# Gate normalisation in PSUM, factor sums on GpSimd, and stored outputs gated one behind each addition

## The chip, the cores and the metric

One NeuronCore of a Trainium2 chip runs the whole program in one launch. The metric is the device time in microseconds; three runs of the kernel before took 2028.3, 2031.29 and 2031.46 us, so the median is 2031.29 us. Each engine works through its own queue in order: TensorE (PE: matmuls, and PEld: loads of its weights), VectorE (DVE), ScalarE (ACT), GpSimd (POOL) and SyncE (SP, which issues all DMAs here). Results of matmuls land in PSUM, which GpSimd cannot be given as an operand here; everything else is in SBUF.

## The reference

Attention in which every query keeps its 32 largest scores, and on its output a mixture of 8 experts. The weights of the experts for each token come from a matrix that is normalised over rows and columns in turn, 8 times (Sinkhorn), so every token uses every expert, and no expert's share is known before the last token's attention is done.

```python
scores = scale * q @ k.T                      # 4 batches, 8 heads, 576 x 576, head size 64
kth = np.partition(scores, -32)[..., -32]     # keep the 32 largest of a row
attn = softmax(where(scores >= kth, scores, -1e9))
x = (attn @ v) as 2304 x 512
P = np.exp(x @ w_gate - max)                  # 2304 x 8
for _ in range(8):
    P /= P.sum(1, keepdims=True) + 1e-09
    P /= P.sum(0, keepdims=True) + 1e-09
    P *= N / E
for e in range(8):
    out += P[:, e:e + 1] * (np.maximum(x @ w1[e], 0.0) @ w2[e])   # w1: 512 x 1024, w2: 1024 x 512
```

## The kernel before

The tokens form 18 tiles of 128 rows. Tiles 0 to 9 (five blocks, `BOARD`) go through the experts while attention for later tokens still runs; since the gate is not known yet, their 80 outputs (10 tiles, 8 experts) are copied to DRAM by `output` without their gate factor. Tiles 10 to 17 (`LAST`) go through the experts after attention. All matmuls of the experts work on values split in two: a high half rounded to the matmul's format (`hi_act`, on ScalarE) and a low half, the difference (`lo_pool` on GpSimd or `lo_dve` on VectorE), in three products: high by high, high by low, low by high. Every weight tile, 128 x 1024, is loaded by SP (`wr`), its high half `wh` made by ScalarE and its low half `wl` by GpSimd.

When the last attention stage is done, `gate_logits` has left all logits in `lg`, and `sinkhorn` makes `P` of them, 128 partitions x 18 tiles x 8 experts: the row sums and both divisions are VectorE's, the sum over the 128 partitions is a matmul with a matrix of ones into PSUM (line 381). Then the PSUM and SBUF pools of attention are closed, and those of the last phase (`psx`, `x2`, `h2`, `cp_`) take their place, so the first matmuls into `pb` and `pc` come after the last round.

`right_factors` prepares the last 8 tiles for a product of 2 x 2 blocks with seven products instead of eight (Strassen's scheme in Winograd's form): B11, B21, B22 are blocks of x, T1 to T4 are differences of blocks, 512 columns x 2 each, and each of the seven is split into halves. `left_factors` does the same to each w1 tile: four sums S1 to S4 on GpSimd (line 593), and the split of the tile and of the sums.

The last phase is 16 half visits, two for each expert. A half visit is two `hidden_pair` (seven products of 6 matmuls, line 607, then ReLU and the split of h into `h2h` and `h2l`) and `last_outputs`: for each of the 8 tiles, 12 matmuls (line 666) into a `p2` bank, of which there are two, and an addition on VectorE, `acc = p2 * P + acc` (line 515, the first time line 513). After each of the half visits 2 to 11, `finish` takes one of tiles 0 to 9: eight times it loads a stored output into a `y` slot (there are four, `YB`) and adds it to an `acc` in the same way, then it stores the `acc`.

The order on each engine is made by a scheduler ahead of the run: it takes the program as traced, the priorities (`tc.high_priority`) and its own model of durations, and lists each engine's instructions; on the chip each queue runs in that order and waits at semaphores. So `finish` can be moved up by it, ahead of what was traced before, as soon as its operands exist.

Of the kernel before, what the change touches and what calls it, by code (L numbers as in the profile page):

```python
# [7 lines left out]
F32 = mybir.dt.float32  # L8
F32R = mybir.dt.float32r
AF = mybir.ActivationFunctionType  # L10
OP = mybir.AluOpType
# [3 lines left out]
DM, E, F = 512, 8, 1024  # L15
N = NB * S
NT = N // 128
# [10 lines left out]
BLOCKS = [[("t", b, 2 * p), ("t", b, 2 * p + 1)] for b in range(NB) for p in range(2)]  # L28
# [3 lines left out]
BOARD = [0, 4, 8, 12, 16]  # L32
# [7 lines left out]
WR, WB, XR, NS, RAW, YB = 3, 6, 3, 3, 3, 4  # L40
# [3 lines left out]
def kernel(  # L44
# [11 lines left out]
    nc = tc.nc  # L56
# [3 lines left out]
    const = ctx.enter_context(tc.tile_pool(name="const", bufs=1))  # L60
    wp = ctx.enter_context(tc.tile_pool(name="wp", bufs=2))
    op_ = ctx.enter_context(tc.tile_pool(name="op", bufs=2))
# [6 lines left out]
    pss = actx.enter_context(tc.tile_pool(name="pss", bufs=1, space=PSUM))  # L69
    pst = actx.enter_context(tc.tile_pool(name="pst", bufs=2, space=PSUM))  # L70
# [3 lines left out]
    def hi_act(dst, src):  # L74
        nc.scalar.activation(dst, src, AF.Copy)  # L75
# [4 lines left out]
    def lo_pool(dst, src, hi):  # L80
        nc.gpsimd.tensor_tensor(dst, src, hi.bitcast(F32), op=OP.subtract)  # L81

    def lo_dve(dst, src, hi):
        nc.vector.tensor_tensor(dst, src, hi.bitcast(F32), op=OP.subtract)  # L84
# [8 lines left out]
    P = const.tile([128, NT, E], F32, name="P")  # L93

    tile_id = {p: i for i, p in enumerate(p for blk in BLOCKS for p in blk)}

    def store_rows(eng, src, piece):
        kind, a, b = piece
        if kind == "t":
            r = a * S + b * 128  # L100
            eng.dma_start(out[r:r + 128, :], src)
        else:
            for i, bb in enumerate((a, b)):
                r = bb * S + 512
                eng.dma_start(out[r:r + 64, :], src[i * 64:(i + 1) * 64])

    spill = {}
# [251 lines left out]
    ones = const.tile([128, 128], F32, name="ones")  # L359
    nc.vector.memset(ones, 1.0)  # L360

    def sinkhorn():
        lgf = lg.rearrange("p t e -> p (t e)")
        mx = const.tile([128, 1], F32, name="mx")
        nc.vector.reduce_max(mx, lgf, axis=mybir.AxisListType.X)
        tp = pst.tile([128, 512], F32, name="pt")
        nc.tensor.transpose(tp[:, 0:128], mx.to_broadcast([128, 128]), idt)
        nmx = const.tile([128, 1], F32, name="nmx")
        nc.vector.reduce_max(nmx, tp[:, 0:128], axis=mybir.AxisListType.X)
        nc.vector.tensor_scalar(nmx, nmx, -1.0, None, op0=OP.mult)  # L370
        nc.scalar.activation(P.rearrange("p t e -> p (t e)"), lgf, AF.Exp, bias=nmx)
        rs = const.tile([128, NT], F32, name="rs")
        cs = const.tile([128, E], F32, name="cs")
        for _ in range(8):
            nc.vector.reduce_sum(rs, P, axis=mybir.AxisListType.X)
            nc.vector.tensor_scalar(rs, rs, 1e-9, None, op0=OP.add)
            nc.vector.reciprocal(rs, rs)
            nc.vector.tensor_tensor(P, P, rs[:, :, None].to_broadcast([128, NT, E]), op=OP.mult)
            nc.vector.reduce_sum(cs, P.rearrange("p t e -> p e t"), axis=mybir.AxisListType.X)
            cp = pst.tile([128, 512], F32, name="pt")  # L380
            nc.tensor.matmul(cp[:, 0:E], ones, cs, start=True, stop=True)
            cr = const.tile([128, E], F32, name="cr")
            nc.vector.tensor_scalar(cr, cp[:, 0:E], 1e-9, None, op0=OP.add)
            nc.vector.reciprocal(cr, cr)
            nc.vector.tensor_scalar(cr, cr, float(N // E), None, op0=OP.mult)
            nc.vector.tensor_tensor(P, P, cr[:, None, :].to_broadcast([128, NT, E]), op=OP.mult)

    ACC = {}

# [119 lines left out]
    def add_output(t, y, e):  # L509
        g = P[:, t, e:e + 1]  # L510
        if t not in ACC:
            ACC[t] = cp_.tile([128, 512], F32, name="acc", bufs=10)
            nc.vector.tensor_scalar(ACC[t], y, g, None, op0=OP.mult)
        else:
            nc.vector.scalar_tensor_tensor(ACC[t], y, g, ACC[t], op0=OP.mult, op1=OP.add)  # L515

    def finish(pieces):
        for piece in pieces:
            t = tile_id[piece]
            for e in range(E):  # L520
                y = op_.tile([128, 512], F32, name="y", bufs=YB)
                nc.sync.dma_start(y, spill[t, e])
                add_output(t, y, e)
            store_rows(nc.sync, ACC[t], piece)

    def right_factors(tm):
        def rows(kh):

            for c, (a, b) in enumerate(((5, 7), (6, 8))):
                cs = slice(c * 256, c * 256 + 256)
                x1 = block_rows(a)[:, 2 * kh:2 * kh + 2, :]
                if BLOCKS[b][0][0] == "t":
                    yield cs, x1, block_rows(b)[:, 2 * kh:2 * kh + 2, :]
                else:
                    for i, piece in enumerate(BLOCKS[b]):
                        ms = slice(c * 256 + i * 128, c * 256 + i * 128 + 128)
                        yield ms, x1[:, :, i * 128:i * 128 + 128], X[piece][:, 2 * kh:2 * kh + 2, :]

        def block_rows(blk):
            x = X[BLOCKS[blk][0]]
            return bass.AP(tensor=x.tensor, offset=x.offset, ap=[list(p) for p in x.ap[:-1]] + [[1, 256]])

        def factor(name):
            return [x2.tile([128, 2, 512], F32R, name=f"{name}{p}", bufs=1) for p in "hl"]

        def split(name, parts):
            h, l = factor(name)
            for cs, src in parts:  # L550
                hi_act(h[:, :, cs], src)
                lo_dve(l[:, :, cs], src, h[:, :, cs])
            return h, l

        def temp():
            return tm.tile([128, 2, 512], F32, name="tf", bufs=4)

        def sub(dst, a, b):
            nc.vector.tensor_tensor(dst, a, b, op=OP.subtract)

        top, low = list(rows(0)), list(rows(1))
        f = {}
        f["B11"] = split("B11", [(cs, a) for cs, a, _ in top])
        t1, t2 = temp(), temp()
        for cs, a, b in top:
            sub(t1[:, :, cs], b, a)
        f["T1"] = split("T1", [(slice(0, 512), t1)])
        f["B21"] = split("B21", [(cs, a) for cs, a, _ in low])
        for cs, _, b in low:
            sub(t2[:, :, cs], b, t1[:, :, cs])  # L570
        f["T2"] = split("T2", [(slice(0, 512), t2)])
        t3 = temp()
        for (cs, _, b1), (_, _, b2) in zip(top, low):
            sub(t3[:, :, cs], b2, b1)
        f["T3"] = split("T3", [(slice(0, 512), t3)])
        f["B22"] = split("B22", [(cs, b) for cs, _, b in low])
        t4 = temp()
        for cs, a, _ in low:
            sub(t4[:, :, cs], a, t2[:, :, cs])
        f["T4"] = split("T4", [(slice(0, 512), t4)])  # L580
        return f
# [72 lines left out]
        put(1, 0, u)  # L654
        return hh, hl

    def last_outputs(e, s0, hs):
        ws = [convert(w2[e, s0 + i], [128, 2, 512]) for i in range(2)]
        for ti, piece in enumerate(p for blk in LAST for p in BLOCKS[blk]):
            ts = slice(ti * 128, ti * 128 + 128)  # L660
            ps = ps2.tile([128, 512], F32, name="p2")
            i = 0
            for (hh, hl), (wh, wl) in zip(hs, ws):
                for ft in range(2):
                    for a, m in ((hh, wh), (hh, wl), (hl, wh)):
                        nc.tensor.matmul(ps, a[:, ft, ts], m[:, ft, :], start=(i == 0), stop=(i == 11))  # L666
                        i += 1
            add_output(tile_id[piece], ps, e)
            if e == E - 1 and s0 == 2:
                store_rows(nc.sync, ACC[tile_id[piece]], piece)  # L670

# [2 lines left out]
    factors = {}  # L674
# [23 lines left out]
    first.close()  # L698
    h2 = ctx.enter_context(tc.tile_pool(name="h2", bufs=3))
    cp_ = ctx.enter_context(tc.tile_pool(name="cp", bufs=2))  # L700
    spilled = [p for blk in range(len(BOARD)) for p in BLOCKS[blk]]
    for e in range(E):
        for s0 in (0, 2):
            last_outputs(e, s0, [hidden_pair(e, s0 + i, factors) for i in range(2)])
            if 2 * e + s0 // 2 >= 2:
                finish(spilled[:1])
                del spilled[:1]


# [55 lines left out]
```

## Time and profile before

| | us |
|---|---|
| median of three runs | 2031.29 |
| lowest, highest | 2028.3, 2031.46 |
| the profiled execution | 2030.8 |
| its span, first to last instruction | 2029.0 |
| TensorE busy | 1901.4 |
| VectorE busy | 1534.8 |
| GpSimd busy | 1079.9 |
| ScalarE busy | 1045.0 |

The profile is one execution. Its rows call the engines PE, PEld, DVE, ACT, POOL and SP; `L515` is line 515 of the kernel; `acc<-y,P,acc` names output and inputs of an instruction; `x70` is a count. `<-` in a list of waits reads "waited for". PEclk is the clock that TensorE was granted as a share of full speed, 2.4 GHz.

### The profile page before, as it was taken

Reading aid. Unit: us, or ns where it says so; the run is one execution under the profiler, and the core shown is the slowest. Engines: PE = TensorE matmul, PEld = TensorE weight load, DVE = VectorE, ACT = ScalarE, POOL = GpSimd, SP = SyncE. Lnnn points to the kernel's source line nnn. Section 1 sums busy time; section 2 is a strip of 40 time slices with the busy share of each in tenths; the row PEclk is TensorE's granted clock in tenths of the full one; section 3 lists DMA queues with packets and bytes.
Section 4 is the critical chain, followed back from the end, with each engine's and each line's share of the span. In section 5 each row is a group of like instructions: output and inputs, shape, how many; then the busy total and the mean of one; then the engine's idle time right before and its main releaser. Section 6 shows DMA issues by size and latency. Waiting matters only on the chain.

```text
span 2029.0 us, 27288 instructions
## 1 busy us (share of the span) xinstructions
PE 1901.4 (94%) x9571; PEld 1586.7 (78%) x9571; DVE 1534.8 (76%) x2861; ACT 1045.0 (52%) x1715; POOL 1079.9 (53%) x953
## 2 busy tenths in 40 slices
PE   4798789999999999999999999879889999999998
PEld 3676678888888887878888888667668888888887
DVE  8999999999999999946999993857893333333333
ACT  5766667657656656645656666423222333333331
POOL 4547866655545544535545556834444454355530
PEclk9899989999999999999999999989899999999999
DMA  3476545443333333324333335414661111111111
GB/s 112 143 246 222 186 165 165 150 155 115 107 124 120 115 114 107 120 102 156 113 106 119 118 115 167 135 52 150 215 205 42 46 59 63 42 42 52 63 42 42
DMA packets 95785, 238.97 MB, mean 118 GB/s; under 512 B 10784, under 2 KB 12960, under 8 KB 95648
## 3 DMA queue, kind: packets, MB, share of 16 engines
q1 hardware_dynamic: 95648, 237.23, 36.3%
q8 instruction: 75, 1.23, 0.3%
q14 instruction: 62, 0.51, 0.1%
HBM read 203.11 MB, written 34.08 MB: 117 GB/s over the span
## 4 chain that ended last, share of the span: by engine, by line
PE 52%; DVE 38%; DMA 5%; issue 3%; ACT 1%; POOL 1%; SPq 0%; DVEq 0%; ACTq 0%; POOLq 0%
PE p L666 15%; DVE m L136 11%; PE p L497 10%; DVE w L143 9%; PE p L410 9%; PE p L607 7%; DVE Et L145 5%; PE pc L607 4%; DVE hl L460 3%; DVE acc L515 3%; DVE atl L84 2%; PE pb L607 2%; DMA y<-y 2%; DMA wr<-in_w_dram 1%; PE pt L233 1%
## 5 line engine op out<-in xcount | busy, mean ns | idle before, releaser
L81 POOL TENSOR_TENSOR wl<-wr,wh 128x1024 fp32r<-128x1024 f32 x280 | 687.5, 2466 | 531.5 <-ACT wh L75 522.5
L75 ACT ACTIVATE wh<-wr 128x1024 fp32r<-128x1024 f32 x280 | 294.3, 1059 | 254.0 <-PE p L607 164.5
L136 DVE MAX8 m<-w 128x8 f32<-128x576 f32 x432 | 318.5, 750 | 1.7
L410 PE MATMUL p<-xh,wh 128*128 128x256 f32 (+1 forms) x768 | 265.6, 346 | 14.8 <-DVE hl L460 8.5
L410 PE MATMUL p<-xl,wh 128*128 128x256 f32 (+1 forms) x768 | 262.7, 342 | 0.0
L410 PE MATMUL p<-xh,wl 128*128 128x256 f32 (+1 forms) x768 | 262.3, 342 | 0.0
L497 PE MATMUL p<-wh,hl 128*128 128x512 f32 x640 | 249.0, 400 | 9.6 <-DVE hl L460 9.6
L497 PE MATMUL p<-wh,hh 128*128 128x512 f32 x640 | 253.5, 400 | 0.5 <-ACT hh L459 0.5
L497 PE MATMUL p<-wl,hh 128*128 128x512 f32 x640 | 251.9, 397 | 0.5 <-POOL wl L81 0.5
L666 PE MATMUL p<-wh,h2h 128*128 128x512 f32 x512 | 203.5, 397 | 12.1 <-DVE acc L515 11.4
L143 DVE MATCH_REPLACE8 w<-m,w 128x576 f32<-128x576 f32 x288 | 213.8, 744 | 0.2
L666 PE MATMUL p<-wh,h2l 128*128 128x512 f32 x512 | 199.3, 395 | 6.7 <-DVE h2l L631 6.7
L666 PE MATMUL p<-wl,h2h 128*128 128x512 f32 x512 | 201.9, 394 | 0.0
L515 DVE SCALAR_TENSOR_TENSOR acc<-p,P,acc 128x512 f32<-128x512 f32 x120 | 88.7, 749 | 147.6 <-PE p L666 147.6
L145 DVE SCALAR_TENSOR_TENSOR Et<-s,m,Et 128x576 f32<-128x576 f32 x144 | 164.2, 1148 | 17.0 <-ACT Et L139 16.2
L410 PEld LDWEIGHTS p<-xh,wh 128*128 128x128 f32 x768 | 147.4, 192 | 36.9 <-DVE hl L460 9.4
L410 PEld LDWEIGHTS p<-xl,wh 128*128 128x128 f32 x768 | 147.5, 192 | 14.5
L410 PEld LDWEIGHTS p<-xh,wl 128*128 128x128 f32 x768 | 147.5, 192 | 14.5 <-issue 0.4
L497 PEld LDWEIGHTS p<-wh,hl 128*128 128x128 f32 x640 | 121.0, 190 | 34.1 <-DVE hl L460 11.6
L497 PEld LDWEIGHTS p<-wl,hh 128*128 128x128 f32 x640 | 121.9, 191 | 24.1 <-POOL wl L81 0.9
L497 PEld LDWEIGHTS p<-wh,hh 128*128 128x128 f32 x640 | 121.8, 191 | 23.6 <-ACT hh L459 1.4
L152 ACT ACTIVATE Et<-Et,st 128x576 f32<-128x576 f32 x144 | 105.0, 771 | 57.4 <-DVE st L150 57.2
(179 smaller groups left out, 4105.2 us busy)
## 6 DMA issues: line engine op xcount, KB each, us to landing
wr<-in_w_dram SPq DMA_DIRECT2D x240, 512.0 KB, 3.5
y<-y SPq DMA_DIRECT2D x160, 256.0 KB, 3.1
raw<-in_k_dram SPq DMA_DIRECT2D x56, 288.0 KB, 3.1
wr<-in_w_dram SPq DMA_DIRECT2D x48, 256.0 KB, 3.5
raw<-in_q_dram SPq DMA_DIRECT2D x32, 256.0 KB, 3.0
p<-y SPq DMA_DIRECT2D x32, 256.0 KB, 3.3
y<-p SPq DMA_DIRECT2D x32, 256.0 KB, 4.1
raw<-in_v_dram SPq DMA_DIRECT2D x28, 288.0 KB, 2.9
```

Source lines behind the costliest of these rows:

```text
L75: nc.scalar.activation(dst, src, AF.Copy)
L81: nc.gpsimd.tensor_tensor(dst, src, hi.bitcast(F32), op=OP.subtract)
L136: nc.vector.max(m8[u][:, r, :], ws[u] if r else s)
L143: nc.vector.match_replace(ws[u], m8[u][:, r, :], ws[u] if r else s, LOWEST)
L145: nc.vector.scalar_tensor_tensor(Em, s, m8[u][:, 3, 7:8], Em, op0=OP.is_ge, op1=OP.mult, accum_out=rsum)
L152: nc.scalar.activation(Et[:, i, :], Et[:, i, :], AF.Copy, scale=st[:, 1, i:i + 1])
L410: nc.tensor.matmul(ps[:, fo, :], a[:, kk, fs], x[:, k0 + kk, cs], start=(i == 0), stop=(i == 3 * nk - 1))
L460: nc.vector.scalar_tensor_tensor(seat.hl[:, ft, cs], src, 0.0, seat.hh[:, ft, cs].bitcast(F32), op0=OP.max, op1=OP.subtract)
L497: nc.tensor.matmul(ps, a[:, ft, ts], m[:, ft % 2, :], start=(i == 0), stop=(i == 3 * NFT - 1))
L515: nc.vector.scalar_tensor_tensor(ACC[t], y, g, ACC[t], op0=OP.mult, op1=OP.add)
L607: nc.tensor.matmul(ps, w[:, kk, :], x[:, kk, :], start=(fresh and i == 0), stop=(i == 5), skip_group_check=True)
L666: nc.tensor.matmul(ps, a[:, ft, ts], m[:, ft, :], start=(i == 0), stop=(i == 11))
```

## The change

There are three parts. (1) `sinkhorn` keeps the gate matrix, the row sums and the scaled column sums in one PSUM tile, `bank`, the one that held attention scores; the reciprocals `rs` and `cr` and the partial sums `cs` stay in SBUF. The addition of 1e-9 and the factor N/E become one instruction, so a round has eight instructions on VectorE instead of nine. The last round writes `P` in SBUF. (2) In `right_factors` the differences and all low halves go from VectorE to GpSimd. (3) `finish` becomes a generator, `stored`, which gives one stored output at each call; `last_outputs` calls it after each of its additions, and `tc.issue_after` makes the VectorE instruction of that call come after the addition in VectorE's queue. So ten half visits, from the first, gate 8 stored outputs each.

```diff
--- before.py
+++ after.py
@@ -368,22 +368,25 @@
         nmx = const.tile([128, 1], F32, name="nmx")
         nc.vector.reduce_max(nmx, tp[:, 0:128], axis=mybir.AxisListType.X)
         nc.vector.tensor_scalar(nmx, nmx, -1.0, None, op0=OP.mult)
-        nc.scalar.activation(P.rearrange("p t e -> p (t e)"), lgf, AF.Exp, bias=nmx)
+
+        bank = pss.tile([128, 2, 512], F32, name="sp")
+        Q = bank[:, 0, 0:NT * E].rearrange("p (t e) -> p t e", t=NT)
+        rp, cp = bank[:, 0, 256:256 + NT], bank[:, 0, 320:320 + E]
+        nc.scalar.activation(bank[:, 0, 0:NT * E], lgf, AF.Exp, bias=nmx)
         rs = const.tile([128, NT], F32, name="rs")
         cs = const.tile([128, E], F32, name="cs")
-        for _ in range(8):
-            nc.vector.reduce_sum(rs, P, axis=mybir.AxisListType.X)
-            nc.vector.tensor_scalar(rs, rs, 1e-9, None, op0=OP.add)
-            nc.vector.reciprocal(rs, rs)
-            nc.vector.tensor_tensor(P, P, rs[:, :, None].to_broadcast([128, NT, E]), op=OP.mult)
-            nc.vector.reduce_sum(cs, P.rearrange("p t e -> p e t"), axis=mybir.AxisListType.X)
-            cp = pst.tile([128, 512], F32, name="pt")
-            nc.tensor.matmul(cp[:, 0:E], ones, cs, start=True, stop=True)
-            cr = const.tile([128, E], F32, name="cr")
-            nc.vector.tensor_scalar(cr, cp[:, 0:E], 1e-9, None, op0=OP.add)
-            nc.vector.reciprocal(cr, cr)
-            nc.vector.tensor_scalar(cr, cr, float(N // E), None, op0=OP.mult)
-            nc.vector.tensor_tensor(P, P, cr[:, None, :].to_broadcast([128, NT, E]), op=OP.mult)
+        cr = const.tile([128, E], F32, name="cr")
+        for i in range(8):
+            nc.vector.reduce_sum(rp, Q, axis=mybir.AxisListType.X)
+            nc.vector.tensor_scalar(rp, rp, 1e-9, None, op0=OP.add)
+            nc.vector.reciprocal(rs, rp)
+            nc.vector.tensor_tensor(Q, Q, rs[:, :, None].to_broadcast([128, NT, E]), op=OP.mult)
+            nc.vector.reduce_sum(cs, Q.rearrange("p t e -> p e t"), axis=mybir.AxisListType.X)
+            ct = pst.tile([128, 512], F32, name="pt")
+            nc.tensor.matmul(ct[:, 0:E], ones, cs, start=True, stop=True)
+            nc.vector.tensor_scalar(cp, ct[:, 0:E], 1e-9, float(E) / N, op0=OP.add, op1=OP.mult)
+            nc.vector.reciprocal(cr, cp)
+            nc.vector.tensor_tensor(P if i == 7 else Q, Q, cr[:, None, :].to_broadcast([128, NT, E]), op=OP.mult)
 
     ACC = {}
 
@@ -510,18 +513,19 @@
         g = P[:, t, e:e + 1]
         if t not in ACC:
             ACC[t] = cp_.tile([128, 512], F32, name="acc", bufs=10)
-            nc.vector.tensor_scalar(ACC[t], y, g, None, op0=OP.mult)
-        else:
-            nc.vector.scalar_tensor_tensor(ACC[t], y, g, ACC[t], op0=OP.mult, op1=OP.add)
-
-    def finish(pieces):
-        for piece in pieces:
-            t = tile_id[piece]
-            for e in range(E):
-                y = op_.tile([128, 512], F32, name="y", bufs=YB)
-                nc.sync.dma_start(y, spill[t, e])
-                add_output(t, y, e)
-            store_rows(nc.sync, ACC[t], piece)
+            return nc.vector.tensor_scalar(ACC[t], y, g, None, op0=OP.mult)
+        return nc.vector.scalar_tensor_tensor(ACC[t], y, g, ACC[t], op0=OP.mult, op1=OP.add)
+
+
+    def stored(piece):
+        t = tile_id[piece]
+        for e in range(E):
+            y = op_.tile([128, 512], F32, name="y", bufs=YB)
+            nc.sync.dma_start(y, spill[t, e])
+            add_output(t, y, e)
+            if e == E - 1:
+                store_rows(nc.sync, ACC[t], piece)
+            yield
 
 
 
@@ -549,14 +553,14 @@
             h, l = factor(name)
             for cs, src in parts:
                 hi_act(h[:, :, cs], src)
-                lo_dve(l[:, :, cs], src, h[:, :, cs])
+                lo_pool(l[:, :, cs], src, h[:, :, cs])
             return h, l
 
         def temp():
             return tm.tile([128, 2, 512], F32, name="tf", bufs=4)
 
         def sub(dst, a, b):
-            nc.vector.tensor_tensor(dst, a, b, op=OP.subtract)
+            nc.gpsimd.tensor_tensor(dst, a, b, op=OP.subtract)
 
         top, low = list(rows(0)), list(rows(1))
         f = {}
@@ -654,7 +658,7 @@
         put(1, 0, u)
         return hh, hl
 
-    def last_outputs(e, s0, hs):
+    def last_outputs(e, s0, hs, more):
         ws = [convert(w2[e, s0 + i], [128, 2, 512]) for i in range(2)]
         for ti, piece in enumerate(p for blk in LAST for p in BLOCKS[blk]):
             ts = slice(ti * 128, ti * 128 + 128)
@@ -665,7 +669,9 @@
                     for a, m in ((hh, wh), (hh, wl), (hl, wh)):
                         nc.tensor.matmul(ps, a[:, ft, ts], m[:, ft, :], start=(i == 0), stop=(i == 11))
                         i += 1
-            add_output(tile_id[piece], ps, e)
+            added = add_output(tile_id[piece], ps, e)
+            with tc.issue_after(added.ins):
+                next(more, None)
             if e == E - 1 and s0 == 2:
                 store_rows(nc.sync, ACC[tile_id[piece]], piece)
 
@@ -698,13 +704,10 @@
     first.close()
     h2 = ctx.enter_context(tc.tile_pool(name="h2", bufs=3))
     cp_ = ctx.enter_context(tc.tile_pool(name="cp", bufs=2))
-    spilled = [p for blk in range(len(BOARD)) for p in BLOCKS[blk]]
+    more = (x for blk in range(len(BOARD)) for p in BLOCKS[blk] for x in stored(p))
     for e in range(E):
         for s0 in (0, 2):
-            last_outputs(e, s0, [hidden_pair(e, s0 + i, factors) for i in range(2)])
-            if 2 * e + s0 // 2 >= 2:
-                finish(spilled[:1])
-                del spilled[:1]
+            last_outputs(e, s0, [hidden_pair(e, s0 + i, factors) for i in range(2)], more)
 
 
 # ---- launch: one core; inputs laid out for the kernel, output as the reference has it ----
```

GpSimd's queue around the new work. Before, from the last splits of weights (`wl`) for the visits to the first sums (line 593) and splits for `hidden_pair`:

```order
L81 TENSOR_TENSOR wl<-wr,wh 128x1024 x18
L593 TENSOR_TENSOR wr<-wr 128x256 x2
L81 TENSOR_TENSOR wl<-wr,wh 128x1024
L593 TENSOR_TENSOR wr<-wr 128x256 x5
L81 TENSOR_TENSOR wl<-wr,wh 128x1024 x2
```

The same place now, where `tf` are the differences and line 597 is what 593 was; ahead of these rows stand two differences and the low halves of B11, B21 and most of B22:

```order
L81 TENSOR_TENSOR T1l<-tf,T1h 128x1024
L81 TENSOR_TENSOR B22l<-xm,B22h 128x2x128
L81 TENSOR_TENSOR wl<-wr,wh 128x1024 x3
L563 TENSOR_TENSOR tf<-xt,tf 128x2x256
L81 TENSOR_TENSOR T3l<-tf,T3h 128x1024
L563 TENSOR_TENSOR tf<-xt,tf 128x2x128 x2
L81 TENSOR_TENSOR T2l<-tf,T2h 128x1024
L81 TENSOR_TENSOR wl<-wr,wh 128x1024 x3
L81 TENSOR_TENSOR T4l<-tf,T4h 128x1024
L81 TENSOR_TENSOR wl<-wr,wh 128x1024 x3
L597 TENSOR_TENSOR wr<-wr 128x256 x7
L81 TENSOR_TENSOR wl<-wr,wh 128x1024 x2
```

The last nine weight splits ahead of the sums now stand behind and between the factor work; two of the five sums that stood behind the first split for `hidden_pair` now stand ahead of the second.

VectorE's queue in the finishing stretch. Before, where additions of stored outputs (`acc<-y`) begin to stand among those of the current half visit (`acc<-p`):

```order
L515 SCALAR_TENSOR_TENSOR acc<-y,P,acc 128x512 x3
L515 SCALAR_TENSOR_TENSOR acc<-p_14332,P,acc 128x512
L515 SCALAR_TENSOR_TENSOR acc<-y,P,acc 128x512
L636 TENSOR_TENSOR pb<-p_14419,t 128x512
L513 TENSOR_SCALAR acc<-y,P 128x512
L515 SCALAR_TENSOR_TENSOR acc<-y,P,acc 128x512 x2
```

Now, in the second half visit:

```order
L517 SCALAR_TENSOR_TENSOR acc<-p_14302,P,acc 128x512
L516 TENSOR_SCALAR acc<-y,P 128x512
L517 SCALAR_TENSOR_TENSOR acc<-p_14320,P,acc 128x512
L517 SCALAR_TENSOR_TENSOR acc<-y,P,acc 128x512
L640 TENSOR_TENSOR pc<-pc,t 128x512
L640 TENSOR_TENSOR pb<-pb,t 128x512
L635 SCALAR_TENSOR_TENSOR h2l<-pc,h2h 128x512
L517 SCALAR_TENSOR_TENSOR acc<-p_14337,P,acc 128x512
L517 SCALAR_TENSOR_TENSOR acc<-y,P,acc 128x512
```

Stored and current additions alternate, one to one, in the first ten half visits.

SP's queue. Before, in the finishing stretch, loads of stored outputs (`y`) and the store of a finished tile (line 101) follow each other with few weight loads between; afterwards weight loads (`wr`) come in pairs:

```order
L522 DMA y<-y_7_13820 128x512
L392 DMA wr<-in_w_dram 128x1024
L101 DMA out_dram<-acc 128x512
L585 DMA wr<-in_w_dram 128x1024 x2
L392 DMA wr<-in_w_dram 128x1024 x2
```

Now, one of the ten half visits, where line 589 loads a w1 tile and line 395 a w2 tile:

```order
L524 DMA y<-y_4_4674 128x512
L524 DMA y<-y_5_5018 128x512
L524 DMA y<-y_6_5362 128x512
L524 DMA y<-y_7_5706 128x512
L524 DMA y<-y_0_7920 128x512
L524 DMA y<-y_1_8204 128x512
L589 DMA wr<-in_w_dram 128x1024
L524 DMA y<-y_2_8488 128x512
L101 DMA out_dram<-acc 128x512
L524 DMA y<-y_3_8772 128x512
L395 DMA wr<-in_w_dram 128x1024 x2
L589 DMA wr<-in_w_dram 128x1024
```

The weight loads of these half visits stand among loads that wait for a `y` slot, and two of them behind a store that waits for the eighth addition of a stored output.

On TensorE's queue the eight column sums move up among the last visits; the second, third and fourth of them stand in a row, behind two matmuls of a group whose third needs the low half of its weights.

## Rows read from the trace of the kernel before

**Rows 1.** The page, parts 1 and 2: busy shares; TensorE and its clock in 40 slices.

```profile
PE 1901.4 (94%) x9571; PEld 1586.7 (78%) x9571; DVE 1534.8 (76%) x2861; ACT 1045.0 (52%) x1715; POOL 1079.9 (53%) x953
...
PE   4798789999999999999999999879889999999998
...
PEclk9899989999999999999999999989899999999999
```

**Rows 2.** Busy time by stretch: stretch, its length, then each engine with its instruction count.

```profile
1262.40:1340.00 77.60, 56.27 (x291) 48.00 (x291) 64.06 (x110) 30.49 (x45) 50.54 (x27) 0.85 0.33 111
...
1390.00:1520.00 130.00, 112.52 (x439) 86.76 (x438) 117.46 (x135) 34.79 (x51) 58.04 (x36) 0.92 0.69 218
...
1600.00:2000.00 400.00, 400.00 (x1740) 326.15 (x1739) 149.73 (x214) 131.50 (x190) 185.27 (x128) 1.00 0.14 47
```

**Rows 3.** Who waited for whom, 1388 to 1530 us: total, times, longest, in us.

```profile
PE p L666 <- DVE acc L515: 10.7, 8, 2.8
PE p L666 <- DVE h2l L631: 6.7, 3, 3.4
```

**Rows 4.** Instruction groups of VectorE, 1388 to 1520 us: count, busy us, mean ns, idle before.

```profile
L515 DVE SCALAR_TENSOR_TENSOR acc<-y,P,acc 128x512 f32<-128x512 f32 x70 | 79.5, 1138 | 9.6 <-DMA y<-y 8.4 <-DVE h2l L631 0.3
L515 DVE SCALAR_TENSOR_TENSOR acc<-p,P,acc 128x512 f32<-128x512 f32 x18 | 13.2, 744 | 0.0
```

**Rows 5.** VectorE in order of time, from 1388 us: start, duration in us.

```profile
1391.04 2.31 DVE L515 SCALAR_TENSOR_TENSOR acc<-y,P,acc 128x512 f32<-128x512 f32 x1
```

**Rows 6.** Who waited for whom, 1262 to 1340 us, waits of TensorE.

```profile
PE pt L381 <- DVE cs L379: 13.2, 4, 4.0
PE p L497 <- DVE hl L460: 5.7, 1, 5.7
PE p L410 <- DVE hl L460: 2.1, 1, 2.1
```

**Rows 7.** Matmuls of line 607 alone, in three stretches.

```profile
1312.00:1320.00 8.00, 4.57 (x18) 3.18 (x18) 0.94 0.91 276
1320.00:1332.50 12.50, 0.00 (x0) 0.00 (x0) 0.50 0.18 68
1332.50:1340.00 7.50, 7.45 (x24) 5.64 (x24) 0.76 0.00 0
```

**Rows 8.** Busy time in two short stretches of the transition.

```profile
1273.30:1279.00 5.70, 0.00 (x0) 0.00 (x0) 5.70 (x4) 0.54 (x1) 5.70 (x3) 0.92 0.25 92
1279.00:1284.50 5.50, 5.47 (x13) 4.31 (x14) 5.50 (x3) 1.58 (x2) 4.12 (x2) 0.50 0.65 200
```

**Rows 9.** GpSimd in order of time, 1255 to 1335 us.

```profile
1261.80 2.41 POOL L81 TENSOR_TENSOR wl<-wr,wh 128x1024 fp32r<-128x1024 f32 x1 [1.88 <-ACT wh L75]
1267.26 15.86 POOL L81 TENSOR_TENSOR wl<-wr,wh 128x1024 fp32r<-128x1024 f32 x4 [3.06 <-ACT wh L75]
...
1322.31 2.95 POOL L593 TENSOR_TENSOR wr<-wr 128x256 f32<-128x256 f32 x4
```

**Rows 10.** VectorE in order of time, 1262 to 1334 us.

```profile
1272.72 3.18 DVE L84 TENSOR_TENSOR T1l<-tf,T1h 128x1024 fp32r<-128x1024 f32 x1
...
1284.79 1.21 DVE L84 TENSOR_TENSOR T2l<-tf,T2h 128x1024 fp32r<-128x1024 f32 x1
...
1299.74 0.17 DVE L383 TENSOR_SCALAR cr<-pt 128x8 f32<-128x8 f32 x1 [0.54 <-PE pt L381]
...
1300.18 2.23 DVE L385 TENSOR_SCALAR cr<-cr 128x8 f32<-128x8 f32 x1
...
1329.69 0.31 DVE L386 TENSOR_TENSOR P<-P,cr 128x144 f32<-128x144 f32 x1
...
1332.96 0.31 DVE L386 TENSOR_TENSOR P<-P,cr 128x144 f32<-128x144 f32 x1
```

**Rows 11.** The page, parts 5 and 6: weight halves on ScalarE; DMA issue to landing, us.

```profile
L75 ACT ACTIVATE wh<-wr 128x1024 fp32r<-128x1024 f32 x280 | 294.3, 1059 | 254.0 <-PE p L607 164.5
...
wr<-in_w_dram SPq DMA_DIRECT2D x240, 512.0 KB, 3.5
y<-y SPq DMA_DIRECT2D x160, 256.0 KB, 3.1
```

## The prediction

> **What bounds the kernel now.** I read the page's busy shares and slices first, then the stretches, then who waited for whom, then the timelines of the engines waited for. The page shows a kernel bound by TensorE: busy 94% of 2029.0 us, its clock at full speed in nearly every slice, so a gain can only come from where TensorE stands or runs slow [rows 1]. Two places near the gate are such.
>
> The first is the finishing stretch, 1390 to 1520 us, in which `finish` adds the 80 stored outputs. From 1600 to 2000 us TensorE retires 1740 matmuls in 400 us, 4.35 per us, without a gap; this is the same mixture of `hidden_pair` and `last_outputs`, without stored outputs. From 1390 to 1520 it retires 439 where that rate gives 565.5 [rows 2]. The 126.5 missing ones are 126.5 / 4.35 = 29.1 us: 17.5 us idle (130 - 112.52), the other 11.6 us at a granted clock of 0.92 on average. The waits name VectorE, 10.7 us for the additions that free the `p2` banks and 6.7 us for the low halves of h [rows 3]. VectorE is 90% busy there (117.46 of 130), because 70 of the additions take 1138 ns each, against 744 ns for those that read PSUM [rows 2, 4].
>
> The second is the transition, 1262 to 1340 us, from the last gate logits to the first full `hidden_pair`. TensorE does 56.3 us of work in 77.6 us: 21.3 us idle [rows 2]. It waits 5.7 and 2.1 us for the low half of h, which stands on VectorE behind the factor sums, and 13.2 us for the column sums of the Sinkhorn rounds [rows 6]. 18 matmuls of line 607 are done by 1320 us, none in the next 12.5 us, then 24 in 7.5 us [rows 7]. The clock suffers as well: after 5.7 us without a matmul the next 13 take 5.5 us at a granted 0.50 [rows 8], the lower level, 1.2 GHz.
>
> **The change part by part.** Gate matrix in PSUM. A round before takes 3.27 us when nothing disturbs it (1329.69 to 1332.96) [rows 10]. Disturbed, its small steps stretch: the same kind of instruction on 8 columns took 0.17 us with its source in PSUM and 2.23 us from SBUF [rows 10]. The change puts the sources in PSUM and drops one 8-column step. I take 3.3 us a round; bounds 3.1 (one 0.17 step less) and 5.8 (eight rounds in the 46 us from 1287, where the factor sums end, to 1333.3). The rounds start earlier too, at about 1269, since VectorE no longer does the factor work first: the exponent stands on ScalarE behind the T1 split, which waits for the first difference.
>
> Factor work on GpSimd. By the order it is seven low halves and four differences, each 1024 columns in one to three pieces. A 1024-column piece takes 2.41 us, four of 256 columns 2.95, so 0.74 each, and 512 columns by the line between them 1.29 [rows 9]. In three pieces (512 and twice 256) that is 2.77. T1 to T4: 4 x 2.41 = 9.6; B11, B21, B22: 3 x 2.77 = 8.3; the differences: 4 x 2.77 = 11.1. GpSimd gains 29.0 us of work, and VectorE loses it. It cannot hide there: by the order it stands ahead of the weight splits that TensorE's last visits need. GpSimd is free at 1264.2 (1261.80 + 2.41) [rows 9]. Ahead of the first split of the sums S1 to S4 there stand the 29.0 us, nine weight splits (21.7) and seven sums (5.2); with the split itself (2.4) it is done at 1264.2 + 58.3 = 1322.5. On the way, the first 19.0 us of factor work make TensorE wait until about 1285.6; three column sums stand in a row in TensorE's queue at that place and wait two rounds, 6.6 us, at the same time, so this is counted once. The last round ends near 1304, ahead of the first use of what it frees (about 1309), so normalisation leaves the path. By the order TensorE has issued 20 matmuls of `hidden_pair` when it needs the split that is done at 1322.5. Before, 18 are done at 1332.5 and 42 at 1340 [rows 7]. From 1322.5 at 4.35 per us the 42nd falls at 1327.6: 12.4 us earlier. I take off 1.4 us for a clock that may be low after the waits, and take **11 us**.
>
> Bounds of this: GpSimd's pace is the unknown. Beside VectorE's factor work four splits took 15.86 us, 3.97 each instead of 2.41, while T1's low half on VectorE took 3.18 instead of the 1.21 of T2's [rows 9, 10]. At that pace 58.3 us become 96 and the transition loses 27 us. The other end is a TensorE that waits for nothing: 21.3 us idle and some 4.6 us of slow clock come back, 26 us. I stay with 2.41, since the instructions that stretched it are those that leave VectorE. [...]
>
> Stored outputs, one behind each addition. The same 80 additions and loads, spread over ten half visits instead of crowded into three. A half visit is 180 matmuls, 41.4 us. VectorE is 37% busy in the steady part (149.73 of 400), 15.5 us per half visit, and gets 8 x 1.14 = 9.1 us more: 59% [rows 2, 4]. Additions come 12 matmuls, 2.76 us, apart; a pair takes 0.74 + 1.14 = 1.9 us. Where GpSimd is in the way a stored one took 2.31 us [rows 5], and the pair 3.05: 0.3 us too long, which the second `p2` bank covers once. Queued behind a late one are the next `p2` addition and the low halves of h. I take 2 us as lost in all, bounds 0 and 24 (80 times 0.3). A load lands 3.1 us after its issue [rows 11], and its slot is freed four additions, 11 us, ahead. So **27 us** come back.
>
> **Sum.** 2029.0 - 27 - 11 = 1991 us of span. The profiled execution took 2030.8 us, 1.8 above its span, and the median of the three runs is 0.5 above that: 1993 us.
>
> **Rivals.** GpSimd becomes the bound. For it: 29 us of work placed ahead of weight splits that were nearly continuous, and small rounds that stretch if the row and column factors left in SBUF still collide. Against it: the 2.41 us rows. With nothing gained in the transition the time is 2004, with the full 27 us lost 2031.
>
> Stored additions still hold TensorE. For it: GpSimd is busy 46% of the steady part (185.27 of 400) [rows 2], so many pairs meet a split. Against it: the mean of 1138 ns already holds such meetings. At 24 us instead of 2 the time is 2015.
>
> The transition gains all: TensorE finds work while GpSimd is late, 26 us instead of 11, 1978 us.
>
> Slower than before: the weights come late. SP's queue is in order; in the new order one w1 load stands behind six loads of stored outputs, and both w2 loads stand behind the store of a finished piece, which waits for its eighth addition. If SP fell that far behind, a w2 half would be ready 3.5 + 1.06 + 2.41 = 7 us after that addition, the second 2.4 us later [rows 9, 11]. It decides from 3.8 us per half visit on (38 us over ten); at 5 us the time is 2043. Against it: those loads are for the half visit that starts some 41 us later.
>
> That the change does not do what it says is excluded by the order: the additions alternate, and the differences are on GpSimd.
>
> **Chances.** Forecast, 1985 to 2003: 0.62. GpSimd the bound: 0.13. Stored additions: 0.10. All gained: 0.10. Weights late: 0.03. The rest, 0.02, is no change. The range 1980 to 2012 leaves out half of the all-gained case, the upper parts of the GpSimd and the stored cases, and the weights. What a measurement of this kernel can tell from no change is about 0.2%, 4 us: faster 0.95, same 0.02, slower 0.03.
>
> **What would show it.** Right: from some 1340 us on a steady 4.35 matmuls per us at a granted clock of 1.00, stored additions until about 1760 us; the eight rounds at 3.3 us; weight splits at 2.4 us; TensorE's waits between 1275 and 1325 named for GpSimd and the column sums. Wrong: splits near 4 us, waits of line 670 for VectorE's additions, a TensorE waiting for w2, or a first split of the sums well off 1322 us.

## The result, and the profile after

The changed kernel takes 1987.18 us, the median of 4 runs (1985.03 to 1987.53), against 2031.0 us for the kernel before: 0.9784 of its time, interval 0.977 to 0.9798, 43.8 us less. The forecast of 1993 us was 5.8 us too long; the time lies in the stated range, and in the forecast's own (1985 to 2003). The profiled execution has a span of 1982.8 us, 46.2 less than before.

Not all of the 46.2 us belong to the change. The last copy of gate logits (line 333 in both kernels) starts here, where the columns are the least, median and longest duration in ns, then the first and the last start in us; first the kernel before, then the changed one:

```profile
L333 ACT ACTIVATE lg<-pt x10: 167/184/193, 146.0 to 1262.6; 128x16 f32<-128x16 f32 x8, 128x8 f32<-128x8 f32 x2
```

```profile
L333 ACT ACTIVATE lg<-pt x10: 165/184/193, 146.4 to 1260.0; 128x16 f32<-128x16 f32 x8, 128x8 f32<-128x8 f32 x2
```

The changed kernel gets there 2.6 us earlier. The profiles of the twelve kernels of the experiments, all with the same code up to there, spread from 1259.7 to 1265.0 us, so this is taken as the spread of executions. From that copy to the end of the span it is 766.4 us before and 722.8 after: 43.6 us, as in the medians. The experiments below use this measure, called "after the gate"; it comes from one profiled execution of each kernel.

The stretches of the changed kernel, to be set beside [rows 2]; columns as there:

```profile
1262.40:1340.00 77.60, 68.95 (x344) 58.78 (x343) 30.37 (x86) 36.18 (x51) 76.11 (x57) 0.93 0.33 109
1390.00:1520.00 130.00, 130.00 (x567) 106.18 (x566) 68.89 (x95) 43.52 (x63) 62.83 (x42) 1.00 0.34 105
1600.00:1760.00 160.00, 160.00 (x697) 130.67 (x696) 84.31 (x115) 53.75 (x77) 83.79 (x56) 1.00 0.33 100
```

From 1390 to 1520 us TensorE now retires 567 matmuls, the full rate (565.5), where it retired 439; VectorE falls from 117.5 to 68.9 us there and rises to 84.3 of 160 (53%) in the steady part. The waits of [rows 3] are gone. From 1340 us to the end, TensorE waits twice:

```profile
PE p L670 <- ACT h2h L634: 0.7, 1, 0.7
PE p L670 <- DVE acc L517: 0.6, 1, 0.6
```

The stored additions, from 1340 to 1800 us, by groups as in [rows 4]:

```profile
L517 DVE SCALAR_TENSOR_TENSOR acc<-y,P,acc 128x512 f32<-128x512 f32 x70 | 68.8, 982 | 0.0
L517 DVE SCALAR_TENSOR_TENSOR acc<-p,P,acc 128x512 f32<-128x512 f32 x81 | 60.7, 750 | 109.6 <-PE p L670 109.6
```

They take 982 ns each instead of 1138, and never wait for data (idle 0.0); the last starts at 1744.7 us.

In the transition, TensorE's waits of 5.7 and 2.1 us for low halves of h [rows 6] are gone, and the column sums cost 7.1 us instead of 13.2:

```profile
PE pt L386 <- DVE cs L384: 7.1, 3, 2.4
PE pc L611 <- ACT wh L75: 0.7, 1, 0.7
PE pc L611 <- POOL wl L81: 0.6, 1, 0.6
PE p L413 <- POOL wl L81: 0.2, 1, 0.2
```

The rounds on VectorE, in order of time (start, duration, idle before):

```profile
1266.29 0.32 DVE L380 TENSOR_REDUCE sp<-sp 128x18 f32<-128x144 f32 x1 [0.53 <-ACT sp L375]
...
1275.15 0.31 DVE L384 TENSOR_REDUCE cs<-sp 128x8 f32<-128x144 f32 x1
1276.10 0.17 DVE L387 TENSOR_SCALAR sp<-pt 128x8 f32<-128x8 f32 x1 [0.64 <-PE pt L386]
...
1278.91 0.17 DVE L387 TENSOR_SCALAR sp<-pt 128x8 f32<-128x8 f32 x1 [0.48 <-PE pt L386]
...
1281.94 0.17 DVE L387 TENSOR_SCALAR sp<-pt 128x8 f32<-128x8 f32 x1 [0.69 <-PE pt L386]
...
1301.27 0.31 DVE L389 TENSOR_TENSOR P<-sp,cr 128x144 f32<-128x144 f32 x1
```

No step is stretched, beside a GpSimd that never stands still. The rounds shown take 2.8 and 3.0 us; where the column sum stands behind products in TensorE's queue a round takes up to 7.6, and the eight of them 35.3, 4.4 on average. The eighth ends at 1301.6 instead of 1333.3. GpSimd, in order of time:

```profile
1261.54 1.29 POOL L563 TENSOR_TENSOR tf<-xt 128x512 f32<-128x512 f32 x1
...
1279.65 7.03 POOL L81 TENSOR_TENSOR wl<-wr,wh 128x1024 fp32r<-128x1024 f32 x3
...
1315.51 4.75 POOL L81 TENSOR_TENSOR wl<-wr,wh 128x1024 fp32r<-128x1024 f32 x2
```

The first factor work starts at 1261.54; the first split of the sums (half of the 4.75) is done at 1317.9. The first weight split behind factor work is done at 1282.0, and TensorE stands, apart from two pairs of column sums, from about 1276 to 1282:

```profile
1281.30 0.60 PE L386 MATMUL pt<-cs,ones 128*128 128x8 f32 x2 [2.43 <-DVE cs L384]
1282.08 0.58 PE L413 MATMUL p<-xh,wl 128*128 128x256 f32 x1 [0.18 <-POOL wl L81]
```

The column sums and that split end this stand within 0.2 us of each other, and for the first split of the sums TensorE waits 0.6 us (`pc` above). So GpSimd ends TensorE's waits, but by little. Line 611 (607 before) alone, as in [rows 7]:

```profile
1300.00:1320.00 20.00, 7.30 (x29) 5.19 (x30) 0.97 0.50 161
1320.00:1322.00 2.00, 2.00 (x10) 1.63 (x10) 1.00 0.53 209
1322.00:1322.50 0.50, 0.50 (x3) 0.38 (x2) 1.00 0.82 139
```

29 + 10 + 3: the 42nd matmul falls at 1322.5 instead of 1340 us, 14.9 us earlier counted from the logits.

### The profile page after: what moved, and what is told of

Read it like the earlier page. It is cut to its first block, busy times and chain, and to the rows that moved or that the text cites. A ratio compares the mean times of both kernels' runs of the same rounds, so it can differ in the third digit from the quotient of the medians.

```text
span 1982.8 us, 27234 instructions
## 1 busy us (share of the span) xinstructions
PE 1886.4 (95%) x9571; PEld 1581.2 (80%) x9571; DVE 1478.0 (75%) x2828; ACT 1045.3 (53%) x1715; POOL 1100.1 (55%) x978
## 4 chain that ended last, share of the span: by engine, by line
PE 55%; DVE 34%; POOL 3%; DMA 3%; issue 2%; ACT 2%; SPq 0%; POOLq 0%; ACTq 0%; DVEq 0%
PE p L670 18%; DVE m L136 11%; DVE w L143 9%; PE p L611 9%; PE p L500 8%; PE p L413 8%; DVE Et L145 5%; PE pc L611 4%; DVE hl L463 4%; DVE atl L84 3%; PE pb L611 2%; POOL wl L81 2%; DMA wr<-in_w_dram 1%; PE pt L233 1%; DMA raw<-in_q_dram 1%
```

## The experiments: each part alone, and each left out

Six kernels have one or two of the three parts. With the two that exist this is every combination. The edit of each part is its hunk of the diff above; one line stands for each here:

```diff
+        nc.scalar.activation(bank[:, 0, 0:NT * E], lgf, AF.Exp, bias=nmx)   # gate matrix in PSUM
+            nc.gpsimd.tensor_tensor(dst, a, b, op=OP.subtract)   # factor work, with lo_pool
+            with tc.issue_after(added.ins):   # stored outputs spread
```

| parts | median us | ratio to before, interval | after the gate |
|---|---|---|---|
| none | | | 766.4 |
| gate matrix | 2022.98 | 0.9965 (0.995 to 0.998) | 759.0 |
| factor work | 2032.61 | 1.002 (1.001 to 1.003) | 768.9 |
| stored outputs | 2003.02 | 0.9871 (0.9855 to 0.9886) | 736.7 |
| gate matrix, factor work | 2015.92 | 0.9931 (0.9917 to 0.9944) | 752.1 |
| gate matrix, stored outputs | 1993.4 | 0.9825 (0.9808 to 0.9842) | 727.2 |
| factor work, stored outputs | 2004.28 | 0.9875 (0.9862 to 0.9889) | 738.6 |
| all | 1987.18 | 0.9784 (0.977 to 0.9798) | 722.8 |

The intervals come from the medians, the last column from one execution each. Against the kernel before in the same runs the medians give 6.0, -3.7, 25.9, 13.7, 35.6, 25.3 and 43.8 us less, in the order of the table; the last column differs from these by up to 3.8 us, so smaller differences in it show a direction at most.

Stored outputs alone. Expected:

> Kernel before with the stored outputs spread, one behind each addition, alone. Theory: the finishing stretch retires 4.35 matmuls per us throughout, 29 us less: 2002 us; the transition stays as it was, 18 matmuls of hidden_pair by 1320 us and the next at 1332.5. Rival (the additions were cheap after the change only because of the other parts): VectorE's stored additions take over 1.1 us, TensorE waits for them, and only 20 us come: 2011 us.

Measured: 2003 us, 25.9 us less by the medians and 29.7 after the gate, and 567 matmuls from 1390 to 1520 us; the stored additions take 975 ns, so the rival falls. On top of the gate matrix, the factor work or both it gives 31.8, 30.3 and 29.3: it stands by itself. Whether the finer calls would keep the additions apart without `tc.issue_after` was not tested.

The gate matrix alone. Expected:

> Kernel before with the gate matrix in PSUM alone (factor work stays on VectorE, stored outputs stay in finish). Theory (short rounds): the rounds still start at about 1287 us, behind the factor sums, but take 3.0 us each (as in the trace after) and end near 1312 instead of 1333; the 12.5 us without a matmul of hidden_pair go, the waits of 5.7 and 2.1 us for low halves of h stay. About 12 us less: 2019 us. Rival (VectorE's load, not the place of the operands, stretches the rounds): rounds stay near 5.8 us, no gain, 2031 us.

Measured: 2023 us; 7.4 us less after the gate (6.0 by the medians), not 12. The steps are short, but the last round ends at 1325, not 1312:

```profile
1312.33 0.17 DVE L387 TENSOR_SCALAR sp<-pt 128x8 f32<-128x8 f32 x1 [4.96 <-PE pt L386]
...
1324.65 0.31 DVE L389 TENSOR_TENSOR P<-sp,cr 128x144 f32<-128x144 f32 x1
```

VectorE waits 4.96 us for one column sum, which stands in TensorE's queue behind products. The theory priced the steps and left out that queue; the rival is wrong as well.

The factor work alone. Expected:

> Kernel before with the factor work on GpSimd alone (gate matrix stays in SBUF). Theory (operands in SBUF collide with GpSimd): the rounds start near 1268 us but take 5 us or more beside a GpSimd that is never idle, and end near 1312; TensorE waits for column sums all along; 5 to 10 us less, about 2023 us. Rival 1 (VectorE's own load stretched the rounds): 3.3 us a round, and this part alone gains the 14.9 us that the transition gained: 2016 us. Rival 2 (GpSimd's added work makes the weights late): 2031 us or more.

Measured: 0.2% slower. The rounds do start at 1267.5, but stretch as long as GpSimd runs, and the last ends at 1325.0. TensorE waits, then VectorE and GpSimd in order of time:

```profile
PE pt L381 <- DVE cs L379: 22.6, 6, 7.3
```

```profile
1298.40 0.18 DVE L376 TENSOR_SCALAR rs<-rs 128x18 f32<-128x18 f32 x1
1298.61 0.27 DVE L377 RECIPROCAL rs<-rs 128x18 f32<-128x18 f32 x1
1298.91 0.31 DVE L378 TENSOR_TENSOR P<-P,rs 128x144 f32<-128x144 f32 x1
...
1304.64 0.30 DVE L375 TENSOR_REDUCE rs<-P 128x18 f32<-128x144 f32 x1
1304.98 1.89 DVE L376 TENSOR_SCALAR rs<-rs 128x18 f32<-128x18 f32 x1
1306.90 0.27 DVE L377 RECIPROCAL rs<-rs 128x18 f32<-128x18 f32 x1
1307.20 2.10 DVE L378 TENSOR_TENSOR P<-P,rs 128x144 f32<-128x144 f32 x1
...
1311.87 0.30 DVE L375 TENSOR_REDUCE rs<-P 128x18 f32<-128x144 f32 x1
...
1313.07 0.41 DVE L379 TENSOR_REDUCE cs<-P 128x8 f32<-128x144 f32 x1
...
1315.15 0.30 DVE L375 TENSOR_REDUCE rs<-P 128x18 f32<-128x144 f32 x1
```

```profile
1299.67 4.77 POOL L81 TENSOR_TENSOR wl<-wr,wh 128x1024 fp32r<-128x1024 f32 x2 [1.81 <-ACT wh L75]
1304.39 2.44 POOL L81 TENSOR_TENSOR T4l<-tf,T4h 128x1024 fp32r<-128x1024 f32 x1
1306.80 2.33 POOL L81 TENSOR_TENSOR wl<-wr,wh 128x1024 fp32r<-128x1024 f32 x1
1320.11 4.75 POOL L81 TENSOR_TENSOR wl<-wr,wh 128x1024 fp32r<-128x1024 f32 x2 [10.99 <-ACT wh L75]
```

At 1298 us GpSimd stands idle (its 1.81): the steps take 0.18 and 0.31. At 1305 it runs: the same steps take 1.89 and 2.10. From 1309.1 it stands idle for 11 us, and a round takes 3.3 us (1311.87 to 1315.15). So it is GpSimd that stretched them, and not VectorE's own load: rival 1 falls. The reciprocal (0.27) and the reduction (0.30) never stretch. The Trainium skill's "SBUF — State Buffer", section "Who interferes with whom", says which VectorE instructions can collide with GpSimd: those with two SBUF inputs, and `tensor_scalar` and copies, which can enter a mode with two ports, but not reductions. The trace agrees for `tensor_tensor`, `tensor_scalar` and the reduction; that section does not name the reciprocal, and no copy stands here. The time is rival 2's, but not by its cause: GpSimd keeps its pace (2.33 to 2.44 us a split) and is the one that waits, 10.99 us, while TensorE waits 22.6 us in all for column sums.

The three pairs. Expected:

> The changed kernel with the factor work back on VectorE. Theory: the parts add, 29 + 12 us less than before: 1990 us, so the factor work on GpSimd is worth some 3 us. Rival 1 (the move of the factor work carries the transition): 2002 us. Rival 2 (the move costs, because 29 us of GpSimd stand ahead of the weight splits): under 1985 us.

> The changed kernel with the stored outputs back in finish. Theory (gate matrix and factor work act together, the stored outputs apart from them): the gate matrix alone gave 7 us, the factor work on top of it some 8 us: 15 us less than before, 2014 us; 20 us per 130 lost again in the finishing stretch. Rival (all parts stand alone): 7 us less and 4 us more, 2026 us.

> The changed kernel with the gate matrix back in SBUF. Theory (GpSimd, kept busy by the factor work, holds up the small steps whose operands are in SBUF): rounds of 5 to 7 us while GpSimd works, and the factor work costs 4 us as it did alone: 2029 - 26 + 4 = 2007 us. Rival (it was the place of finish that made the factor work cost): some 1995 us.

Measured: 1993.4, 2015.9 and 2004.3 us. The factor work is worth 4.4 us with the other two parts (727.2 to 722.8), 6.9 on top of the gate matrix alone, and less than nothing without it (2.5 lost). The intervals of the ratios bear out both gains, since they do not overlap, and the loss; beside the stored outputs alone (0.9871 and 0.9875) they show no difference. Its gain hangs on the matrix being in PSUM; the first theory for each pair is right to 3.5 us.

## The experiments: what GpSimd's load decides

Theory: GpSimd's sum of work ahead of the first split of the sums sets the transition. Five kernels shift that work or its order, and a sixth tests one instruction. First the differences back on VectorE:

```diff
-            nc.gpsimd.tensor_tensor(dst, a, b, op=OP.subtract)
+            nc.vector.tensor_tensor(dst, a, b, op=OP.subtract)
```

> The changed kernel with the four differences back on VectorE, the low halves staying on GpSimd. GpSimd sheds 11.1 us ahead of the first split of the sums. Theory (GpSimd's sum of work ahead of that split sets the transition): the split is done 6 to 11 us before 1318 us, TensorE's idle and slow time between 1275 and 1320 shrinks, 5 us less than the changed kernel: 1982 us. Rival 1 (VectorE's differences hold GpSimd up as they did before): no gain, 1987 us. Rival 2 (they put off the rounds, and TensorE waits for column sums): 1990 us or more.

Measured: 1989.5 us, ratio 0.9805 (0.9792 to 0.9818): not faster than the changed kernel, and not told apart from it, so the theory falls and the time does not decide between the rivals. GpSimd had less to do (the pair of splits behind the sums starts 51.9 us after the gate instead of 55.5), and no wait names it any more, but TensorE waited elsewhere. VectorE's row, then TensorE's:

```profile
1279.36 0.67 DVE L463 SCALAR_TENSOR_TENSOR hl<-p,hh 128x512 fp32r<-128x512 f32 x1
```

```profile
1280.09 0.79 PE L500 MATMUL p<-wh,hl 128*128 128x512 f32 x1 [7.65 <-DVE nmx L370]
```

The low half of h (`hl`) stands on VectorE behind 6.17 us of differences; TensorE starts as it is done, after 7.65 us. The profile puts that wait down to `nmx`, the next instruction in VectorE's queue. Then the factors' low halves there:

```diff
-                lo_pool(l[:, :, cs], src, h[:, :, cs])
+                lo_dve(l[:, :, cs], src, h[:, :, cs])
```

> The changed kernel with the factors' low halves back on VectorE, the differences staying on GpSimd. GpSimd sheds 18 us. Theory (GpSimd's sum): up to 8 us less than the changed kernel, 1979 us, as far as VectorE's 1024-column pieces (3.2 us each beside GpSimd) do not put off the rounds. Rival (the rounds and low halves of h queue behind them on VectorE, as in the kernel with all of it there, 1993 us): 1990 us or more.

Measured: 1988.6 us, ratio 0.9801 (0.9787 to 0.9814), 723.9 us after the gate: no difference that can be told, so neither theory nor rival. TensorE waits 4.9 us for column sums and 2.0 for a low half of h, and not for GpSimd. So either half of the factor work on GpSimd gives as much as both, as far as these runs can tell. Next the work as it is, but queued behind three weight splits (`SPLITS` lists them in the order of the program):

```diff
+    with tc.high_priority(offset=BIG), tc.tile_pool(name="tm", bufs=4, side="right") as tm:
+        with tc.issue_after(SPLITS[-6].ins):
+            factors.update(right_factors(tm))
```

> The changed kernel with the factor work queued behind three of the weight splits that it stood ahead of on GpSimd (the work itself is the same). Theory (GpSimd's sum of work ahead of the first split of the sums is the limit): TensorE's 6 us without work at 1276 to 1282 go, but that split is still done near 1318 us and TensorE waits for it instead: no gain, 1987 us. Rival (only the order in GpSimd's queue matters): 6 us idle and 2 us of slow clock come back, 1980 us.

Measured: 1990.3 us, ratio 0.9804 (0.9786 to 0.9823). The stand at 1276 to 1282 us is gone, and TensorE waits later, for GpSimd (the profiled execution is the slowest of the five, 1994.07 us):

```profile
PE p L612 <- POOL wl L81: 3.8, 1, 3.8
PE pt L386 <- DVE cs L384: 3.1, 2, 2.4
PE p L501 <- POOL wl L81: 2.2, 1, 2.2
PE pc L612 <- POOL wl L81: 1.3, 1, 1.3
```

As the theory had it, order moves the wait and does not remove it. Last, the late low halves on VectorE, between the rounds, alone and with the order above and the first sums on VectorE:

```diff
+                (lo_dve if name in ("T2", "T3", "T4") else lo_pool)(l[:, :, cs], src, h[:, :, cs])
...
+            (nc.vector if e == 0 and s < 2 else nc.gpsimd).tensor_tensor(st[:, i], a, b, op=op)
```

> The changed kernel with the low halves of T2, T3 and T4 on VectorE, between the Sinkhorn rounds; 7.3 us less on GpSimd, all of it behind the three weight splits at 1280 us. Theory: the first split of the sums is done 7 us earlier, but TensorE waited for it and its neighbours only 1.3 us, and the stand at 1276 to 1282 us is untouched: 1986 us. Rival (VectorE's 1024-column pieces put off the rounds by 3 us each, and they end behind the first use of what they free): 1990 us.

> Both: three weight splits first, low halves of T2 to T4 on VectorE, and the sums of the first two column pairs on VectorE as well (GpSimd sheds 7.3 and 5.2 us). Theory (order and sum together): the stand at 1276 to 1282 goes and the split of the sums is done by about 1306 us, ahead of its use: 8 us less, 1979 us. Rival (the waits for column sums, 7.1 us, are what is left, and they do not depend on GpSimd): 1985 us or more.

Measured: 1997.7 us (0.9844; 0.9824 to 0.9865) and 1995.7 us (0.983; 0.9811 to 0.985), slower than the changed kernel. The theory missed both; the rivals have the direction, but not the size or the cause, since these waits for column sums do depend on GpSimd. One long instruction stands ahead of each of these waits. The kernel with the low halves alone, VectorE, GpSimd and TensorE:

```profile
1279.89 16.61 DVE L84 TENSOR_TENSOR T3l<-tf,T3h 128x1024 fp32r<-128x1024 f32 x1 [0.51 <-ACT T3h L75]
```

```profile
1293.06 2.37 POOL L81 TENSOR_TENSOR wl<-wr,wh 128x1024 fp32r<-128x1024 f32 x1
1306.52 5.75 POOL L81 TENSOR_TENSOR wl<-wr,wh 128x1024 fp32r<-128x1024 f32 x2 [11.09 <-ACT wh L75]
```

```profile
1299.75 0.59 PE L386 MATMUL pt<-cs,ones 128*128 128x8 f32 x2 [19.76 <-DVE cs L384]
```

T3's low half, 1.21 us undisturbed for its like [rows 10], took 16.61 us and ended at 1296.5, 1.07 us after GpSimd went idle (1295.43). With the order changed it took 14.47 us and ended 1.1 us after GpSimd went idle. To tell a missing turn from a hidden wait for data:

```diff
+                if name == "T3":
...
+                        nc.vector.reciprocal(l[:, :, cs], src)
```

> The kernel with the low halves of T2 to T4 on VectorE, but T3's low half is replaced by the reciprocal of its difference: one operand in SBUF in place of two, the same tiles and elements (so that low half is not computed; only times count). T2's, with two operands, now stands right behind it in VectorE's queue. Theory (an instruction with two SBUF operands gets no turn while GpSimd runs one instruction straight after another): the reciprocal takes 1.2 us or a little more, and T2's low half beside it stretches to many us, until GpSimd next stands idle. Rival 1 (the 16.6 us were a wait of T3's low half for data that the profile does not show): the reciprocal takes over 10 us. Rival 2 (the length is an accident of that one place): both take under 4 us.

Measured, on VectorE and GpSimd:

```profile
1274.60 6.55 DVE L558 RECIPROCAL T3l<-tf 128x1024 fp32r<-128x1024 f32 x1
...
1281.10 14.11 DVE L84 TENSOR_TENSOR T2l<-tf,T2h 128x1024 fp32r<-128x1024 f32 x1
```

```profile
1289.48 4.64 POOL L81 TENSOR_TENSOR wl<-wr,wh 128x1024 fp32r<-128x1024 f32 x2
1299.44 2.38 POOL L81 TENSOR_TENSOR wl<-wr,wh 128x1024 fp32r<-128x1024 f32 x1 [5.31 <-ACT wh L75]
```

T2's low half now takes 14.11 us and ends at 1295.2, 1.1 us after GpSimd went idle (1294.1). Three times in three kernels the end is tied to that, so the missing turn is as good as shown and rival 2 falls. The reciprocal took 6.55 us, not 1.2. By its small forms (0.21 us for 8 columns, 0.27 for 18, so 6 ns per column) 1024 columns cost some 6.3 us; by this estimate 6.55 is its own price and no stretching, and the 1.2 expected was wrong. Rival 1 falls too: no wait of 14 us stood at T3's place.

## Why the prediction was right, point by point

**Stored outputs, 27 us: 29.3 measured** (752.1 to 722.8 after the gate; 29.9 by the ratios 0.9931 and 0.9784), the loss of 29.1 that the missing matmuls gave, whole. The 2 us taken as residual are not there: the pair of additions fits, since the stored one fell to 982 ns. The 24 us bound and its rival (2015 us) are refuted by the 0.6 us wait. No load was late: idle 0.0 ahead of the additions, and no wait for w2.

**Transition, 11 us: 14.3 measured** (766.4 to 752.1). All times of this stretch are 2.6 us earlier than foretold, by the execution; that taken off:

- The rounds were foretold to start at 1269 and end at 1304; 1266.3 + 2.6 and 1301.6 + 2.6 are 1268.9 and 1304.2. A round that did not wait for TensorE's other work took 2.8 to 3.0 us instead of 3.3, under the lower bound of 3.1: that bound counted the step that is gone, but not the sum over tokens, which takes 0.31 us from PSUM and 0.41 from SBUF.
- TensorE's wait for the first weight split to 1285.6: 1282.1 + 2.6 = 1284.7.
- GpSimd's 58.3 us to the first split of the sums: 56.4 (1261.5 to 1317.9), since neighbours overlap by some 0.07 us. Its pieces kept the lower pace, 2.4 us a split, as chosen.
- The 42nd matmul at 1327.6: 1322.5 + 2.6 = 1325.1, 2.5 us early, 1.9 of it GpSimd's. The 1.4 us kept for a low clock were not needed: it was low only behind two stands, to 1282 and to 1296 us (the lower level of 1.2 GHz, where the column ahead of the DMA share says 0.50), and 1.00 from 1302 us on. The slow work was done ahead of the split of the sums, for which TensorE still waited 0.6 us:

```profile
1282.00:1286.00 4.00, 3.92 (x18) 3.92 (x19) 2.03 (x8) 0.13 (x1) 4.00 (x3) 0.50 0.57 152
1298.00:1302.00 4.00, 4.00 (x20) 3.78 (x19) 2.11 (x8) 1.55 (x2) 4.00 (x3) 0.58 0.64 232
```

So the error is two reserves, 2 and 1.4 us, and 1.9 us of GpSimd: 5.3 of the 5.8 us by which the median differs.

**What the text had only by luck.** It gave one sum for the two parts at the gate. The factor work alone costs 2.5 us. GpSimd keeps the lower pace even then; but the steps of the rounds, left in SBUF, stretch beside it, and TensorE waits 22.6 us for column sums. So the move pays only together with the gate matrix in PSUM, and the prediction did not say so. The Trainium skill's "GPSIMD Engine Reference", section 4.1, speaks against such a move: it puts elementwise work on VectorE, GpSimd being about twice as slow with two inputs. The trace agrees on the pace (2.41 us against an undisturbed 1.21 [rows 9, 10]); the move paid all the same (727.2 to 722.8 us) with what it left on VectorE in PSUM.

**The rival "GpSimd becomes the bound"** is half right. It is on the path, as the kernel with another order shows, at the price foretold, but only by 0.2 and 0.6 us: TensorE's waits for column sums, 7.1 us, and its own work end almost with GpSimd's splits. The prediction had the column sums beside the first split, and took the second for the one limit of the end. Four kernels that ease GpSimd gained nothing: two are level with the changed kernel, with TensorE waiting for VectorE instead, and two are slower. None of the versions tried beats it.

## What to carry to other kernels

Price two moves together where one engine's instructions decide the other's pace: here the small steps had to go to PSUM before GpSimd could take more work. Where a stretch retires fewer matmuls than a steady stretch with the same mixture, the missing ones divided by the steady rate estimate the whole loss, clock included; here that gave 29.1 us, against 29.3 measured after the gate, and 25.9 by the medians of the kernel with that part alone. Taking work off a full engine pays only if the engine that gets it has no queue of its own that TensorE waits for, and can read its operands in turn.

## What the runs showed of the hardware that was not expected

While GpSimd runs one SBUF instruction straight behind another, a VectorE instruction with both operands in SBUF can wait through all of them: 16.61, 14.47 and 14.11 us for one of 1.2. It is not always so: with all the low halves on VectorE the same pieces took 2.7 to 3.4 us. What lets VectorE in at one boundary and not at another stays open.
